# Batch 1's q and k loaded early and transposed by DMA in an attention and ResMLP kernel

## The chip, the cores and the metric

The kernel runs on one core of one Trainium2 chip. The metric is the device time of one execution in microseconds (us). Every time is a median of a kernel's executions in the fast state; the traces are of one profiled execution each, whose span is 1 to 4.4 us shorter than the median of the timed runs (the profiled run need not be the median one: for e2 and e5 it is the fastest). The core has five engines that work side by side: PE (matrix products), DVE (VectorE), ACT (ScalarE), POOL (GpSimd) and SP (which here only issues DMA). The profile counts the transfers of all of them against the same 16 DMA engines.

## The reference

Eight batches go through attention with 16 query heads and 4 key/value heads, and then through a ResMLP block whose two large weight matrices are the same for all batches.

```python
# q: (8, 16, 384, 64)   k, v: (8, 4, 384, 64)   all f32; k and v repeated 4 times
attn = softmax(q @ k^T / 8);   x = (attn @ v) as (8, 384, 1024)
a1  = alpha1 * x + beta1
tok = einsum('ts,bsd->btd', w_tok, a1)            # 384 x 384
u   = x + lam * tok
a2  = alpha2 * u + beta2
ch  = relu(a2 @ w_ch1) @ w_ch2                    # 1024 -> 4096 -> 1024
out = u + lam * ch
```

## The kernel before

The program is one long list in which the two layers of batch b (`main`) are interleaved with the attention part of batch b+1 (`side`). Batch 0's attention cannot hide behind anything and forms a prologue of some 42 us. Then comes **the first layer of batch 0** (`h`, to about 91 us), **its second layer** (`ch`, to about 142 us), the first layer of batch 1, and so on. These names are used below.

Weights of the first layer, w1, stream in for every batch in 16 chunks of 512 KiB (as bf16) through five buffers. The second layer's weights, w2, are loaded once, first 2 MB and later pieces of 256 and 512 KiB, between the w1 chunks. All of these are loads that convert f32 to bf16 and are issued by POOL:

```python
    def load_w1(n):                                     # n = 16 * batch + chunk
        if n < B * NCH:
            t = sb.tile([P, NDT, CW * P], bf, tag="w1", name="w1", bufs=RING)   # RING = 5
            c = n % NCH
            nc.gpsimd.dma_start(out=t, in_=w1src[:, :, c * CW * P:(c + 1) * CW * P])
            w1_tiles[n] = t
    # in main(b), behind chunk c of the first layer:
            load_w1(b * NCH + c + RING)
            if b == 0 and 2 <= c < 12:
                load_w2(*((0, 6 + c, 16) if c < 10 else (1, c - 10, 16)))
            if b == 0 and c == 12:
                for i in range(1, 8):
                    load_w2(1, i, 8)
```

Attention needs q and k transposed (`qT`, `kT`). There are two ways: PE multiplies by an identity matrix and an engine copies the result from PSUM, or a transposing DMA ("flip") moves it within SBUF, issued by SP:

```python
    def load_q(b, sts=range(NST)):
        if b not in qrs:
            qrs[b] = sb.tile([P, NST, Hq, D], bf, tag="q_raw", name="q_raw", bufs=1)   # one buffer
        for st in sts:
            nc.gpsimd.dma_start(out=qrs[b][:, st], in_=by_st(q[b])[:, st])

    def flip_k(b):
        nc.sync.dma_start_transpose(out=kT..., in_=k2s[b]...)        # 393 KB
    def flip_q(b):
        nc.sync.dma_start_transpose(out=qT..., in_=qrs[b]...)        # 786 KB
```

Before the change batches 0 and 1 use PE for q, k and the MLP's input a2, and batches 2 to 7 use DMA. For batches 2 and up the loads come at 55% and the flips at 85% of the main part of two batches earlier:

```python
                if not loaded and t > t_all * 0.55:
                    ...place_k(b + 2, ...); load_q(b + 2); load_v(b + 2)
                if not flipped and t > t_all * 0.85:
                    flip_k(b + 2); flip_q(b + 2)
```

Batch 0's q lies in the only `q_raw` buffer until late in the prologue, so batch 1's q cannot load earlier:

```python
        loads = {9: [(load_w1, RING - 1), (load_w2, 0, 0, 2)], 20: [(late_loads,)],   # load_k(1)
                 30: [(load_q, 1)], 37: [(load_v, 1)]}
```

The softmax here doesn't subtract the row's maximum and nothing guards it: scores larger than these inputs give would overflow.

## Time and profile before

| | before |
|---|---|
| time, median of 3 | 815.77 us (815.12 to 817.19) |
| PE busy in the span | 98% |
| first layer of batch 0 ends (first `ch` matmul) | 91.42 us |
| second layer of batch 0 ends (batch 1's first layer starts) | 141.83 us |
| waits of PE within batch 0's first layer, all together | 1.56 us |

The page of the kernel before opens with the busy time of each engine (with share of the span and number of instructions), and its third part lists the DMA queues: records, megabytes, and the time the records took as a share of the span.

```profile
PE 798.4 (98%) x6090; PEld 451.7 (55%) x6144; DVE 347.5 (43%) x678; ACT 225.0 (28%) x298; POOL 185.8 (23%) x230
...
q0 software_dynamic: 197760, 83.28, 89.8%
q1 hardware_dynamic: 62304, 28.00, 14.2%
```

PE seems to be everything here. But the share is an average over 814 us. The queue q0, which carries the weights, moves 83 MB in that time, 102 GB/s; in the prologue and in batch 0's first layer it moves about twice as much and has no pause. The last line is the queue that carries the flips and the outputs. The prediction below reads batch 0 in detail.

### The profile page before, as it was taken

What the parts mean: (1) busy time and instruction counts of PE and PEld (TensorE: products, weight loads), DVE (VectorE), ACT (ScalarE), POOL (GpSimd) and SP (SyncE); (2) the same over time, 40 slices, a digit from 0 to 9 for tenths busy, and PEclk for the clock granted to TensorE, in tenths of its full rate; (3) what the DMA queues carried; (4) which work ended last, traced back from release to release, by engine and by line L of the source; (5) the groups of instructions that cost most, each with busy time, mean ns of one, the idle gap of its engine ahead of it and who ended that gap; (6) DMA issues with size and microseconds to landing.
All of it is one profiled execution on the core that took longest, in us unless ns stands there. A gap on an engine that the chain in (4) does not pass through costs nothing.

```text
span 814.3 us, 14117 instructions
## 1 busy us (share of the span) xinstructions
PE 798.4 (98%) x6090; PEld 451.7 (55%) x6144; DVE 347.5 (43%) x678; ACT 225.0 (28%) x298; POOL 185.8 (23%) x230
## 2 busy tenths in 40 slices
PE   7999999999999999999999999999999999999997
PEld 4756555565456655566455654556555665556545
DVE  7655553344443444334442444424444244442122
ACT  4644330432113321233113331034211432102100
POOL 7244340234003240032301241022500321003000
PEclk8999999999999999999999999999999999999999
DMA  9999999999169991799947999499994998129611
GB/s 174 200 196 201 202 212 140 161 183 166 49 131 172 176 149 56 138 181 174 124 89 128 173 178 96 112 132 174 171 83 99 162 173 122 36 64 187 88 39 39
DMA packets 260670, 112.57 MB, mean 138 GB/s; under 512 B 109568, under 2 KB 254464, under 8 KB 260608
## 3 DMA queue, kind: packets, MB, share of 16 engines
q0 software_dynamic: 197760, 83.28, 89.8%
q1 hardware_dynamic: 62304, 28.00, 14.2%
q8 instruction: 48, 0.79, 0.4%
q10 hardware_dynamic: 544, 0.39, 0.2%
q14 instruction: 14, 0.11, 0.0%
HBM read 170.53 MB, written 12.58 MB: 225 GB/s over the span
## 4 chain that ended last, share of the span: by engine, by line
PE 90%; DMA 4%; DVE 4%; issue 1%; SPq 0%; POOL 0%; ACT 0%; DVEq 0%; ACTq 0%
PE ch L426 41%; PE h L399 37%; PE av L236 4%; PE sc L202 4%; PE tok L258 3%; DMA q_raw<-in_q_dram 2%; DMA w<-in_moe_w_ch_dram 2%; DVE x L242 1%; DVE hT L409 1%; DVE a1f L249 0%; DVE a L251 0%; DMA hT<-in_moe_lam_dram 0%; POOL q_raw L108 0%; SPq L472 0%; PE vec L318 0%
## 5 line engine op out<-in xcount | busy, mean ns | idle before, releaser
L399 PE MATMUL h<-a2T,w 128*128 128x384 bf16 (+1 forms) x2016 | 349.9, 326 | 1.7 <-ACT hT L407 0.5
L426 PE MATMUL ch<-w,hT 128*128 128x512 bf16 (+2 forms) x1546 | 346.1, 370 | 4.4 <-issue 0.9
L399 PEld LDWEIGHTS <-w 128*128 128x128 bf16 x2016 | 189.4, 98 | 126.3 <-issue 9.1
L126 POOL DMA_DIRECT2D w<-in_moe_w_ch_dram x128 | 112.3, 879 | 543.3 <-PE h L399 500.5
L426 PEld LDWEIGHTS <-hT 128*128 128x128 bf16 x1600 | 146.1, 98 | 153.0 <-issue 5.8
L211 ACT ACTIVATE es<-sc 128x1024 bf16<-128x1024 f32 x126 | 123.3, 1021 | 283.2 <-PE sc L202 283.2
L409 DVE TENSOR_SCALAR hT<-h,bias 128x384 bf16<-128x384 f32 x128 | 79.1, 618 | 187.0 <-PE h L399 186.5
L407 ACT ACTIVATE hT<-h,bias 128x384 bf16<-128x384 f32 x128 | 74.2, 580 | 222.1 <-PE h L399 202.6
L431 DVE TENSOR_TENSOR o<-ch,vecs 128x512 f32<-128x512 f32 (+2 forms) x50 | 33.4, 667 | 91.1 <-PE ch L426 91.1
L265 DVE TENSOR_TENSOR x<-tok,x 128x384 f32<-128x384 f32 x64 | 35.6, 556 | 80.9 <-PE tok L258 77.2
L236 PEld LDWEIGHTS <-es 128*128 128x128 bf16 x1008 | 45.8, 97 | 20.5
L236 PE MATMUL av<-v,es 128*128 128x65 bf16 x1008 | 49.0, 193 | 0.0
L202 PE MATMUL sc<-qT,kT 64*128 64x384 bf16 (+2 forms) x576 | 46.0, 275 | 0.4 <-ACT hT L211 0.3
L258 PEld LDWEIGHTS <-wtokT 128*128 128x128 bf16 x576 | 37.8, 98 | 12.6 <-issue 0.6
L241 DVE RECIPROCAL rinv<-av 128x6 f32<-128x6 f32 x64 | 12.3, 193 | 69.8 <-PE av L236 69.6
L258 PE MATMUL tok<-a,wtokT 128*128 128x128 bf16 x504 | 37.3, 219 | 0.0
L242 DVE TENSOR_TENSOR x<-av,rinv 128x384 f32<-128x384 f32 x64 | 35.7, 557 | 2.3
L202 PEld LDWEIGHTS <-kT 64*128 64x128 bf16 x576 | 20.0, 94 | 28.8 <-issue 24.6
L432 DVE TENSOR_TENSOR o<-o,x 128x512 f32<-128x512 f32 (+2 forms) x50 | 33.5, 671 | 1.7
L269 DVE TENSOR_TENSOR a<-x,vecs 128x384 bf16<-128x384 f32 x56 | 31.6, 564 | 1.9
L251 DVE TENSOR_TENSOR a<-a1f,vecs 128x384 bf16<-128x384 f32 x56 | 31.3, 558 | 2.2
L249 DVE TENSOR_TENSOR a1f<-x,vecs 128x384 f32<-128x384 f32 x56 | 31.2, 558 | 1.9
(69 smaller groups left out, 211.5 us busy)
## 6 DMA issues: line engine op xcount, KB each, us to landing
w<-in_moe_w_ch_dram POOLq DMA_DIRECT2D x135, 512.0 KB, 7.2
out_dram<-o SPq DMA_DIRECT2D x47, 256.0 KB, 2.0
q_raw<-in_q_dram POOLq DMA_DIRECT2D x21, 256.0 KB, 8.0
kst<-in_k_dram SPq DMA_DIRECT2D x16, 192.0 KB, 2.8
w<-in_moe_w_ch_dram POOLq DMA_DIRECT2D x10, 256.0 KB, 12.5
w<-in_moe_w_ch_dram POOLq DMA_DIRECT2D x1, 2048.0 KB, 21.9
v<-in_v_dram POOLq DMA_DIRECT2D x21, 64.0 KB, 7.9
a2T<-a SPq DMA_TRANSPOSE x48, 4.2
```

Of the source, the lines that this page charges most:

```text
L126: nc.gpsimd.dma_start(out=t, in_=w1src[:, :, c * CW * P:(c + 1) * CW * P])
L202: nc.tensor.matmul(out=sc[:, hh, k % 4:k % 4 + n], lhsT=kT[r, sk, 2 * p // G, :], rhs=qT[r, st:st + n, p, :], start=True, stop=True)
L211: nc.scalar.activation(out=e, in_=sc, func=EXP, scale=scale_qk)
L236: nc.tensor.matmul(out=av[:, hh, sq, :], lhsT=ess[k // 4][:, hh, k % 4, :], rhs=vb[:, sk, hk, :], start=(sk == 0), stop=(sk == NST - 1))
L242: nc.vector.tensor_tensor(out=x[:, :, cols(p)].rearrange("p st (h d) -> p h st d", h=2), in0=av[:, :, :, :D], in1=rinv.to_broadcast([P, 2, ...
L258: nc.tensor.matmul(out=ps[:, tt, :], lhsT=wtokT[:, st, tt * P:(tt + 1) * P], rhs=a1s[p][:, st, :], start=(st == 0), stop=(st == NST - 1 an ...
L265: nc.vector.tensor_tensor(out=u, in0=ps, in1=u, op=ADD)
L399: nc.tensor.matmul(out=ps[:, :n], lhsT=w1[:, dt, j * P:(j + 1) * P], rhs=a2T[:, dt, :n], start=(dt == 0), stop=(dt == NDT - 1))
L407: nc.scalar.activation(out=hT[:, nt, :], in_=ps[:, :S], func=RELU, bias=c1)
L409: nc.vector.tensor_scalar(out=hT[:, nt, :], in0=ps[:, :S], scalar1=c1, scalar2=0.0, op0=ADD, op1=mybir.AluOpType.max)
L426: nc.tensor.matmul(out=ps[:, lo:hi], lhsT=hT[:, nt, ms * P:(ms + 1) * P], rhs=w2[:, nt, dw * 512 + lo:dw * 512 + hi], start=(nt == 0), sto ...
L432: nc.vector.tensor_tensor(out=o[:, lo:hi], in0=o[:, lo:hi], in1=x[:, ms, c], op=ADD)
```

## The change

The intent is to get batch 1 ready earlier and with less work on PE. Batch 0's q goes into four separate tiles, so that `q_raw` is free at once; batch 1's k, q and v load in the prologue; its q and k are flipped by DMA, and its a2 too, as in the later batches. That takes 60 transposes from PE. Besides, LN1's scale is spread over the partitions directly in f32 rather than through a split into bf16 parts, and the early pieces stand in a new order.

```diff
@@ q_transpose
-                nc.tensor.matmul(out=ps[:, i, :], lhsT=qrs[b][:, i % NST, h:h + 2, :].rearrange("p h d -> p (h d)"),
+                nc.tensor.matmul(out=ps[:, i, :],
+                                 lhsT=qgs[h // G][:, i % NST, h % G:h % G + 2, :].rearrange("p h d -> p (h d)"),
@@ a2_transpose
-            if not pe_flip:
-                nc.sync.dma_start_transpose(...)
-                return
-            ps = tp_ps([P, NST, P])                  # (and the transposes on PE, and the copy)
+            nc.sync.dma_start_transpose(...)
@@ new
+        def spread_g1(ps_, tag):
+            ps = psum.tile([P, 4, P], f32, tag=tag, name="vec", bufs=1)
+            for i, p in enumerate(ps_):
+                nc.tensor.matmul(out=ps[:, i], lhsT=ident_f[:NP, p:p + 1].to_broadcast([NP, P]),
+                                 rhs=rows_f[:NP, :P], start=True, stop=True)
+            nc.vector.tensor_copy(out=g1[...], in_=...)
@@ side(b), b > 0
-            if pe_flip:
-                add(k_transpose, 0)
-                add(q_transpose, 0, 2, "DVE", "av")
-                add(k_transpose, 2)
-                add(q_transpose, 2, 2, "DVE", "av")
...
-                    if pe_flip and j in (1, 3):
-                        add(q_transpose, 4 + 2 * (j // 2))
@@ the end of side(0)   (the table of early pieces is also reordered: cut)
-        for f, *a in ((h_part, (0, 1), range(4)), ...
+        for f, *a in ((flip_q, 1), (place_k, 1, 0), (place_k, 1, 1), (flip_k, 1), (h_part, (0, 1), range(4)), ...
@@ prologue
-        load_q(0, [])
+        qgs = [sb.tile([P, NST, G, D], bf, tag="es", name="qg", bufs=EB) for _ in range(Hkv)]
...
-        loads = {9: [(load_w1, RING - 1), (load_w2, 0, 0, 2)], 20: [(late_loads,)], 30: [(load_q, 1)], 37: [(load_v, 1)]}
+        load_k(1)
+        load_q(1)
+        load_v(1)
+        load_w2(0, 0, 2)
```

Cut are the new order of the loads and copies of batch 0's q, the moved `spread` calls of batch 1, changes of the evicting engine and of one PSUM buffer, and `lead` 0.04 to 0.05.

More of the change, by code (lines that the diff above doesn't have):

```diff
@@ L94, in place_k @@
         copies = [nc.gpsimd.tensor_copy] * 2
-        if b == 1 or b == 0 == i:
-            copies = (nc.vector.tensor_copy, nc.vector.tensor_copy if i else nc.scalar.copy)
+        if b == 1:
+            copies = [nc.scalar.copy] * 2
+        elif b == 0 == i:
+            copies = (nc.vector.tensor_copy, nc.scalar.copy)
         for a in range(2):
@@ L163, in side @@
         first = b == 0
-        pe_flip = b < 2
         def cols(p):
@@ L253, in tok @@
         def tok(p):
-            tag, n = ("mm", 2) if first else ("av", 1) if pe_flip else ("tp", 1)
+            tag, n = ("mm", 2) if first else ("tp", 1)
             ps = psum.tile([P, NST, P], f32, tag=tag, name="tok", bufs=n)
@@ L279, in a2_transpose @@
                 return
-            if not pe_flip:
-                nc.sync.dma_start_transpose(
-                    out=a2T[:, p, :S].rearrange("p (a s) -> p a s", a=NST),
-                    in_=a2s[p].rearrange("p a d -> p (a d)"))
-                return
-            ps = tp_ps([P, NST, P])
-            for tt in range(NST):
-                nc.tensor.matmul(out=ps[:, tt, :], lhsT=a2s[p][:, tt, :], rhs=ident,
-                                 is_transpose=True, start=(tt == 0), stop=(tt == NST - 1),
-                                 skip_group_check=True)
-            nc.scalar.copy(out=a2T[:, p, :S], in_=ps.rearrange("p a b -> p (a b)"))
+            nc.sync.dma_start_transpose(
+                out=a2T[:, p, :S].rearrange("p (a s) -> p a s", a=NST),
+                in_=a2s[p].rearrange("p a d -> p (a d)"))
         def wtok_transpose(st, tag):
@@ L321, in spread @@
                       in_=ps[:, :n * w].rearrange("p (n v) d -> p n v d", n=n))
+        def spread_g1(ps_, tag):
[3 more added lines that the diff above has]
+                                 rhs=rows_f[:NP, :P], start=True, stop=True)
+            nc.vector.tensor_copy(out=g1[:, ps_[0] * P:(ps_[-1] + 1) * P], in_=ps.rearrange("p n d -> p (n d)"))
         us = []
@@ L332, in side @@
         if not first:
-            if pe_flip:
-                add(k_transpose, 0)
-                add(q_transpose, 0, 2, "DVE", "av")
-                add(k_transpose, 2)
-                add(q_transpose, 2, 2, "DVE", "av")
-                if b == 1:
-                    add(split, 2, 4)
+            if b == 1:
+                add(split, 2, 4)
+                for p in (0, 2, 4, 6):
+                    add(spread, (p, p + 1), (1, 3), "av" if p % 4 else "tp", "ACT")
+                for p in (0, 4):
+                    add(spread, range(p, p + 4), (3, 4), "av" if p else "tp", "ACT")
             for j in range(NP + 4):
@@ L345, in side @@
                     add(scores2, j)
-                    if pe_flip and j in (1, 3):
-                        add(q_transpose, 4 + 2 * (j // 2))
                 if 2 < j < NP + 3:
-                    add(tok if pe_flip else tok_flip, j - 3)
-                if pe_flip and j > 3:
-                    add(a2_transpose, j - 4)
-                if b == 1 and j < 2:
-                    for p in (4 * j, 4 * j + 2):
-                        add(spread, (p, p + 1), (1, 3), "tp", "ACT")
-                    add(spread, range(4 * j, 4 * j + 4), (3, 4), "tp", "ACT")
-                elif j < 2:
+                    add(tok_flip, j - 3)
+                if j < 2:
                     us.extend([lambda: None] * 2)
@@ L367, in side @@
         ut = a2_transpose
-        at = {1: [(warmup, 3), (split, 0, 2, 0)], 2: [(q_transpose, 2, 2, "DVE", "av"), (split, 0, 2, 1)],
-              3: [(spread, lower, (0, 1), "tp"), (wtok_transpose, 0, "av")],
-              4: [(av, 0), (wtok_transpose, 1, "tp"), (wtok_transpose, 2, "av")], 5: [(fill_h,), (rows_r, "tp")],
-              6: [(av, 1), (q_transpose, 4, 2)], 7: [(tok, 0), (k_transpose, 2)],
-              8: [(av, 2), (spread, upper, (0, 1), "av")], 9: [(tok, 1), (ut, 0)], 10: [(av, 3), (ut, 1)],
-              11: [(q_transpose, 6, 2), (tok, 2)], 12: [(tok, 3)], 13: [(av, 4), (ut, 2)], 14: [(ut, 3)],
-              15: [(tok, 4), (av, 5)], 16: [(ut, 4)], 17: [(av, 6), (tok, 5)]}
+        at = {0: [(warmup, 3)], 1: [(scale_rows,), (split, 1, 2, 0)], 2: [(q_transpose, 2, 2, "DVE", "av"), (split, 1, 2, 1)],
+              3: [(spread_g1, lower, "tp")], 4: [(wtok_transpose, 0, "av"), (av, 0), (wtok_transpose, 1, "tp")],
+              5: [(wtok_transpose, 2, "av"), (fill_h, 0), (k_transpose, 2)], 6: [(av, 1), (q_transpose, 4, 2)],
+              7: [(rows_r, "av")], 8: [(av, 2), (fill_h, 4)], 9: [(tok, 0), (spread_g1, upper, "av")],
+              10: [(tok, 1), (av, 3)], 11: [(q_transpose, 6, 2), (ut, 0), (tok, 2)], 12: [(tok, 3), (ut, 1)],
+              13: [(av, 4), (ut, 2)], 14: [(ut, 3)], 15: [(tok, 4), (av, 5)], 16: [(ut, 4)], 17: [(av, 6), (tok, 5)]}
         for i in range(18):
@@ L378, in side @@
                 add(f, *a)
-        for f, *a in ((h_part, (0, 1), range(4)), (av, 7), (ut, 5), (tok, 6),
+        for f, *a in ((flip_q, 1), (place_k, 1, 0), (place_k, 1, 1), (flip_k, 1), (h_part, (0, 1), range(4)), (av, 7), (ut, 5), (tok, 6),
                       (h_part, (2, 3), range(4)), (h_part, range(4), (4,)), (ut, 6), (tok, 7),
@@ L404, in main @@
                 if b == 0:
-                    nc.vector.tensor_copy(out=c1, in_=ps[:, S:n])
+                    evac("DVE" if nt % 2 else "ACT")(out=c1, in_=ps[:, S:n])
                 if nt % 2 == 0:
@@ L487, in place_q4 @@
         def place_q4(g, eng):
-            eng.tensor_copy(out=qrs[0][:, :, g * G:(g + 1) * G, :], in_=qhs[g].rearrange("p h st d -> p st h d"))
+            eng.tensor_copy(out=qgs[g], in_=qhs[g].rearrange("p h st d -> p st h d"))
         load_q4(1)
@@ L502, with scale_rows @@
                 nc.vector.tensor_reduce(out=t[:n], in_=ident[:n, :n].rearrange("p (k c) -> p c k", c=NP), op=ADD, axis=AX)
+        def scale_rows():
+            r = rows_f[:, :2 * P].rearrange("p (v d) -> p v d", v=2)
+            nc.vector.tensor_tensor(out=r, in0=r, in1=rows_f[:, None, 3 * P:].to_broadcast([32, 2, P]), op=MUL)
         def split(lo, hi, step=None):
             c = slice(lo * P, hi * P)
-            if lo == 0 and step != 1:
-                r = rows_f[:, c].rearrange("p (v d) -> p v d", v=2)
-                nc.vector.tensor_tensor(out=r, in0=r, in1=rows_f[:, None, 3 * P:].to_broadcast([32, 2, P]), op=MUL)
             for i, m in enumerate(masks[:2]):
@@ L517, in split, with fill_h @@
                 nc.vector.tensor_copy(out=rows_b[:32, c], in_=rows_f[:, c])
-        def fill_h():
-            nc.vector.tensor_tensor(out=H[:32].rearrange("p (n d) -> p n d", n=NP),
-                                    in0=rows_b[:32, None, P:2 * P].to_broadcast([32, NP, P]),
-                                    in1=sel4[:, :, None].to_broadcast([32, NP, P]), op=MUL)
+        def fill_h(p):
+            nc.vector.tensor_tensor(out=H[:32, p * P:(p + 4) * P].rearrange("p (n d) -> p n d", n=4),
+                                    in0=rows_b[:32, None, P:2 * P].to_broadcast([32, 4, P]),
+                                    in1=sel4[:, p:p + 4, None].to_broadcast([32, 4, P]), op=MUL)
         place_k(0, 0)
         for h, cp in ((0, nc.vector.tensor_copy), (2, nc.scalar.copy)):
-            cp(out=qrs[0][:, :, h:h + 2, :], in_=qst[:, h:h + 2].rearrange("p h st d -> p st h d"))
+            cp(out=qgs[0][:, :, h:h + 2, :], in_=qst[:, h:h + 2].rearrange("p h st d -> p st h d"))
         nc.gpsimd.tensor_copy(out=vt[0][:, :, :, :D], in_=vst.rearrange("p h st d -> p st h d"))
@@ L532 @@
         load_q4(3)
-        for c in range(RING - 1):
+        place_k(0, 1)
+        load_w1(0)
+        load_w1(1)
+        place_q4(2, nc.gpsimd)
+        place_q4(3, nc.gpsimd)
+        for c in range(2, RING):
             load_w1(c)
-        place_q4(2, nc.gpsimd)
-        place_k(0, 1)
-        place_q4(3, nc.gpsimd)
         nc.gpsimd.tensor_copy(out=a2Ts[0][:, :, S:S + 1], in_=be2[:, :, None])
-        def late_loads():
-            load_k(1)
-        loads = {9: [(load_w1, RING - 1), (load_w2, 0, 0, 2)], 20: [(late_loads,)], 30: [(load_q, 1)], 37: [(load_v, 1)]}
-        for i, f in enumerate(side(0)):
-            f()
-            for g, *a in loads.get(i, []):
-                g(*a)
-        place_k(1, 0)
-        place_k(1, 1)
+        load_k(1)
+        load_q(1)
+        load_v(1)
+        load_w2(0, 0, 2)
+        for f in side(0):
+            f()
         for b in range(B):
@@ L553 @@
             done, t, loaded, flipped = 0, 0, b + 2 >= B, b + 2 >= B
-            lead, span = (0.04, 0.82) if b == 0 else (0, 0.95)
+            lead, span = (0.05, 0.82) if b == 0 else (0, 0.95)
             if not loaded:
```

## The prediction

> **What bounds the kernel now.** I read the page first: PE is busy 98% of the span and its slices are full after the first. The chain of waits then says where PE is not the whole story. It names matmuls almost everywhere, but before 92 us it also has two long DMA pieces:
>
> ```profile
> 29.02 17.14 DMA q_raw<-in_q_dram
> 74.13 14.07 DMA w<-in_moe_w_ch_dram
> ```
>
> Columns: start, duration, what. The first piece is batch 1's q, issued late because batch 0 still held the one q_raw buffer; it landed at 46.16. The second is the last of the 16 w1 chunks of batch 0; it was 14 us on its way and landed at 88.19. The PE timeline there (start, length, instruction, idle before and its releaser) shows how little this cost:
>
> ```profile
> 45.49 0.28 PE L186 MATMUL tp<-ident,q_raw 128*128 128x128 bf16 x2
> 46.20 0.40 PE L186 MATMUL tp<-ident,q_raw 128*128 128x128 bf16 x4 [0.44 <-DMA q_raw<-in_q_dram]
> ...
> 87.58 0.33 PE L287 MATMUL tp<-ident,a 128*128 128x128 bf16 x3
> 88.24 1.48 PE L399 MATMUL h<-a2T,w 128*128 128x385 bf16 x8 [0.33 <-DMA w<-in_moe_w_ch_dram]
> ```
>
> PE waited only 0.44 and 0.33 us. A small wait at the end of a long transfer means that both sides arrive nearly together. So I asked how full the DMA is, with the table of stretches (length, then busy time of PE, PEld, DVE, ACT, POOL with counts, granted clock, DMA share, GB/s):
>
> ```profile
> 10.00:20.00 10.00, 7.11 (x77) 4.42 (x77) 8.43 (x18) 4.47 (x5) 9.63 (x12) 0.66 1.38 194
> 20.00:30.00 10.00, 9.95 (x160) 7.25 (x161) 8.13 (x18) 8.69 (x11) 3.24 (x3) 1.00 1.40 203
> ...
> 38.00:46.00 8.00, 7.75 (x61) 4.96 (x58) 3.64 (x12) 2.95 (x6) 1.81 (x3) 1.00 2.16 176
> ...
> 52.00:72.00 20.00, 19.30 (x156) 11.54 (x152) 8.59 (x26) 11.56 (x17) 9.61 (x12) 1.00 1.39 200
> 72.00:92.00 20.00, 19.54 (x187) 12.44 (x189) 11.64 (x32) 8.48 (x12) 7.83 (x10) 1.00 1.38 200
> ```
>
> The reader is to see the constant 200 GB/s from 10 us to past 90 us: the DMA is saturated through the whole prologue and batch 0's first layer. The landings of single issues confirm a queue served in order: w1 chunks 12 to 15 landed at 76.43, 80.32, 84.30 and 88.19, one per 3.95 us, which is 512 KiB of w1 plus 256 KiB of w2 (786 KB) at 199 GB/s. PE began them at 77.53, 80.93, 84.45 and 88.24. The slack shrinks from 1.1 us to nothing. Chunk 5 landed at 52.05 and was begun at 53.61, a slack of 1.6 us. **So two limits meet in batch 0's first layer: PE, and the bytes queued ahead of the last w1 chunk.** After about 143 us each batch takes 97.4 us (143.19 to 240.63 in the chain) and the change does not touch those batches.
>
> The same stretch 10 to 20 us shows a granted clock of 0.66, after a PE gap of 2.04 us at 10.02 to 12.06 (released by L517, the splitting of the f32 rows into bf16).
>
> **What the Trainium skill says.** "TensorE: Matmul & The Clock Gate", Part 1: an idle PE is put at half clock, and it takes some 3.4 us of activity to win the full clock back; the trace shows a clock of 0.50 from 14 to 18 us after the gap. Same page, "Wait — 56ns": 128 columns cost 56 ns at full clock; here three transposes step on by 0.17 us (56 ns each), though each record says 219. "DMA: Bandwidth & Descriptors", "Issuing engines are not separate DMA queues": transfers from all issuers run on the same 16 engines and interleave. The trace agrees: around the transposing DMA of one a2 block the w1 queue loses rate. The two queue tables (queue, packets, MB, share), without and with it:
>
> ```profile
> q0 software_dynamic: 1509, 0.76, 143.4%
> ```
>
> ```profile
> q0 software_dynamic: 344, 0.17, 136.2%
> q1 hardware_dynamic: 393, 0.09, 27.5%
> ```
>
> The first is 179 to 183 us (0.19 MB per us of w1). The second is 176.6 to 178.2: 0.17 MB where 0.30 would have passed. The loss of 0.13 MB is 0.7 us of DMA for one block of 98 KB; 186.5 to 188 gives 0.14 against 0.285, again 0.75 us. Alone, the big q flip ran at 208 GB/s (131 to 136 us). The same page, "Latency and other measured facts", gives 261 GB/s or more for transposing DMAs; the trace decides.
>
> **The change part by part.**
>
> (1) Removed from PE: batch 1's k and q transposes (12 + 24) and a2 transposes (24). 60 x 56 ns = 3.4 us. Of these the 36 k/q ones and one a2 group (2.2 us) lie before 91 us, in the first layer; seven a2 groups (7 x 0.17 = 1.2 us) lie in the second layer. Batch 1's work is paced by matmuls issued; counting units of the new list (44, against 54) at the half-way mark, 20 remain for the second layer: 10 half av pieces, 4 scores, 6 tok. Before it was 8, 4, 6 and the transposes. So the second layer changes by +2 x 0.275 - 1.2 = **-0.65 us**.
>
> (2) Prologue: the scale of LN1 is spread directly in f32, so the first av no longer waits for the split; scores fill the old gap. That can recover the 2.0 us gap, and half of some 7 us run at half clock (3 us): **4 to 5 us earlier start** of the first layer (42.5 now, about 38). The f32 spread's extra passes, 8 small matmuls, are about 1 us against that, inside ACT-bound time (18 exps x 1.024 us).
>
> (3) Bytes ahead of the last w1 chunk: the same w1, w2, q, k and v as before, only in another order (q, v now ahead of the first 2 MB of w2). Added: the DMA flips of q (786 KB) and k (393 KB), which the order of SyncE's instructions puts before everything of batch 0's main part, and one of the a2 flips (98 KB) before the last chunk lands. At the rate measured alone (208 GB/s) q and k cost 5.7 us; at the loss measured beside w1 (0.73 us per 98 KB) 8.8 us. I take 7.4, plus 0.7 for the a2 block: **+8 us** on the landing of chunk 15, so about 96.
>
> (4) First layer: PE starts 4 to 5 us earlier, but chunk 5 sits behind q, v, w2 and the flips and lands near 59 instead of 52. PE would reach it near 48, wait some 10 us, then follow the queue at 3.95 us per chunk. The gain of (2) and the 2.2 us of (1) are swallowed by this wait. The layer ends when chunk 15 has landed: +8 us, less the 0.33 us wait already there.
>
> (5) Batch 2's q lands behind the same backlog (129.35 now); its flip ended near 137, 5 us ahead of the scores at 142.57. With seven more a2 flips in the second layer (about 5 us of DMA) that slack is nearly used: +0 to 1 us.
>
> Sum: +7.7 - 0.65 + 0.5, about +7.5. I shade it to **+6.7, or 822.5 us**, because the flips may overlap with w1's reads better than the two small samples say.
>
> **The rivals.** (a) *PE is the bound and DMA is hidden.* Then the time falls by 2.2 + 1.2 of transposes and 4 to 5 of prologue, to about 808. For it: PE's 98%, and waits for DMA under 1 us. Against it: landings and starts that coincide for four chunks in a row, and an unbroken 200 GB/s; no part of the change takes a byte away. (b) *The flips are free*, filling gaps that w1's queue leaves. Then chunk 15 lands at 88 as before and only the -0.65 us remains: about 815. Against it: 0.7 us lost per small block. (c) *The flips cost more,* and batch 2's scores wait for qT: 827 to 830. For it: a clock loss when PE idles 10 us, and SyncE serves outputs and flips in order.
>
> **Range and chances.** The centre is the DMA-bound sum. The low end, 815, is rival (b); the high end, 829, is (c). Rival (a) has about one chance in fifteen. A change of 2% is 16.3 us; faster by that would need more than all idle and transposes of the prologue together, slower by that twice my sum.
>
> **What would show each step.** Right: chunk 15 starts at 94 to 98; the chain before it is a w1 DMA; PE has a hole of several us between 45 and 60, released by w1; 200 GB/s throughout; the second layer takes about 50 us as before (91.58 to 141.99). Step (2): the clock between 12 and 20 us is near 1 and the first-layer matmuls start near 38. Wrong: if PE shows no waits for w1 and chunk 15 starts before 86, DMA was not the bound; if chunk 15 is at 88 with both flips done, they were free.

## The result, and the profile after

The changed kernel took **828.44 us** (median of 4, 826.43 to 829.76), the kernel before 816.14 us in the same rounds. The ratio is 1.0148 (95% interval 1.0122 to 1.0175): slower by 1.5%, within the 2% that counts as the same. Every ratio here is the mean time of one kernel's fast runs over that of the other's in the same rounds, so it is not quite the ratio of the medians quoted.

| | before | after |
|---|---|---|
| first main matmul of batch 0 | 42.54 us | 42.13 us |
| sixth w1 chunk landed (number 5) | 52.05 | 58.24 |
| last w1 chunk of batch 0 landed (number 15) | 88.19 | 99.86 |
| first layer of batch 0 ends | 91.42 | 103.46 |
| second layer of batch 0 ends | 141.83 | 153.76 |
| waits of PE in batch 0's first layer | 1.56 | 14.75 |
| from there to the end | 672.42 | 673.52 |

Nearly all the loss is made before the first layer of batch 0 has ended: +12.0 us there, −0.1 us in the second layer, +1.1 us after it. The same lines of the page of the kernel after:

```profile
PE 798.2 (96%) x6038; PEld 449.0 (54%) x6092; DVE 339.8 (41%) x654; ACT 225.4 (27%) x309; POOL 184.4 (22%) x230
...
q0 software_dynamic: 197760, 83.28, 88.3%
q1 hardware_dynamic: 70304, 29.97, 16.1%
```

q0 moves the same bytes. q1 has 1.97 MB more: q (0.79), k (0.39) and eight blocks of a2 (0.79 together). PE has lost 52 instructions, but no busy time. The chain of waits after the change (start, duration, what) has these pieces of DMA beyond the prologue:

```profile
45.21 22.13 DMA w<-in_moe_w_ch_dram
67.87 16.25 DMA w<-in_moe_w_ch_dram
84.65 15.22 DMA w<-in_moe_w_ch_dram
...
149.42 5.75 DMA qT<-q_raw
```

Three w1 loads in a row carry it, where before there was one of 14 us. The timeline of PE after the change shows what they do to it (in brackets the idle time before and what ended it):

```profile
42.13 1.14 PE L391 MATMUL h<-a2T,w 128*128 128x385 bf16 x6
...
58.29 3.61 PE L391 MATMUL h<-a2T,w 128*128 128x385 bf16 x12 [6.45 <-DMA w<-in_moe_w_ch_dram]
67.39 2.79 PE L391 MATMUL h<-a2T,w 128*128 128x385 bf16 x16 [1.23 <-DMA w<-in_moe_w_ch_dram]
71.31 2.13 PE L391 MATMUL h<-a2T,w 128*128 128x385 bf16 x12 [1.14 <-DMA w<-in_moe_w_ch_dram]
...
99.91 0.83 PE L391 MATMUL h<-a2T,w 128*128 128x385 bf16 x4 [0.83 <-DMA w<-in_moe_w_ch_dram]
...
155.21 0.61 PE L204 MATMUL sc<-qT,kT 64*128 64x384 bf16 x8 [0.64 <-DMA qT<-q_raw]
```

A hole of 6.45 us ends exactly when chunk 5 has landed, and from then on PE waits for nearly every chunk. The stretches of the kernel after (columns as in the prediction):

```profile
10.00:20.00 10.00, 8.72 (x132) 6.04 (x130) 8.88 (x22) 7.92 (x9) 7.59 (x12) 1.00 1.26 182
...
52.00:72.00 20.00, 11.35 (x69) 6.17 (x70) 2.80 (x7) 5.79 (x11) 5.02 (x7) 0.83 1.30 188
72.00:92.00 20.00, 15.63 (x129) 8.61 (x127) 5.96 (x15) 7.58 (x14) 7.81 (x10) 1.00 1.38 200
```

PE did 11.35 us of work where it did 19.30 before, at a clock of 0.83, while the DMA moved 188 and 200 GB/s. What shared the DMA is seen on SP's timeline after the change:

```profile
36.68 11.96 SPq L117 DMA_TRANSPOSE qT<-q_raw  x1
48.74 7.56 SPq L113 DMA_TRANSPOSE kT<-k  x1
```

The two issues lasted 20 us together. With a quiet DMA the same instructions last 4.05 and 1.60 us (batch 2's flips before the change, at 130.99 and 129.28). The queue tables for 54 to 62 us, of the kernel before and then of the kernel after, show the sharing itself:

```profile
q0 software_dynamic: 2661, 1.59, 138.1%
```

```profile
q0 software_dynamic: 1926, 0.99, 88.5%
q1 hardware_dynamic: 1921, 0.48, 46.1%
```

**The two queues got equally many records** (1926 against 1921), and a record of a flip carries 256 bytes where one of the weights carries 512 (0.48 MB over 1921, 0.99 over 1926). So 0.48 MB of flips cost 0.60 MB of weights in these 8 us. This is what the Trainium skill, "DMA: Bandwidth & Descriptors", "Queues, rings and completion order", describes: each DMA engine takes the queue rows that have work in turn, a packet at a time. The trace agrees in so far as the counts are equal; whether a record of the trace is a packet in the page's sense, no run shows.

The flips also came with a slower DMA. Here are two lines of the DMA view of the kernel after for 40 to 68 us, the first with the rate in 40 slices of 0.7 us:

```profile
GB/s 207 195 195 196 196 194 196 200 189 174 147 139 139 126 167 189 87 13 137 183 184 181 184 183 183 182 186 180 184 184 187 188 191 169 200 232 233 240 232 200
DMA packets 10617, 5.02 MB, mean 179 GB/s; under 512 B 4790, under 2 KB 10616, under 8 KB 10616
```

The kernel before moved 5.51 MB in this stretch, 197 GB/s. So the flips not only took 1.18 MB of it, the total fell by 0.49 MB too, above all from 47 to 53 us, where the DMA came nearly to a stop (13 GB/s in one slice) with loads and a flip outstanding. The same stall stands in e2, e3, e5 and e10 (between 48 and 52 us), in every run in which an early flip ran beside loads, and not in the kernel before or in e1. Its cause is not shown.

### The profile page after: what moved, and what is told of

It is laid out like the page before. It is cut to its first block, busy times and chain, and to the rows that moved or that the text cites. A ratio compares the mean times of both kernels' runs of the same rounds, so it can differ in the third digit from the quotient of the medians.

```text
span 827.3 us, 14036 instructions
## 1 busy us (share of the span) xinstructions
PE 798.2 (96%) x6038; PEld 449.0 (54%) x6092; DVE 339.8 (41%) x654; ACT 225.4 (27%) x309; POOL 184.4 (22%) x230
## 4 chain that ended last, share of the span: by engine, by line
PE 87%; DMA 8%; DVE 3%; issue 1%; SPq 0%; ACT 0%; ACTq 0%; POOLq 0%
PE ch L418 39%; PE h L391 35%; DMA w<-in_moe_w_ch_dram 6%; PE sc L204 4%; PE av L238 4%; PE tok L260 4%; DMA qT<-q_raw 1%; DVE x L244 1%; PE h L152 1%; DMA stage<-in_q_dram 1%; PE ut L277 0%; DVE a1f L251 0%; DVE a L253 0%; DVE hT L401 0%; DVE hT L248 0%
## 5 line engine op out<-in xcount | busy, mean ns | idle before, releaser
L243 DVE RECIPROCAL rinv<-av 128x6 f32<-128x6 f32 x64 | 12.3, 193 | 66.0 <-PE av L238 66.0
```

## The experiments

Each kernel was run beside the kernel before on the same chip; all compared runs are fast. The places of time are from the profile of each. "Waits" are those of PE in batch 0's first layer; the last column is from the start of batch 1's first layer to the end. By the rule of 2%, e3 is slower, e6 unclear (its interval spans 2%), and all others count as the same as the kernel before.

| run | time, us | ratio to before (95%) | waits | first layer ends | second ends | rest |
|---|---|---|---|---|---|---|
| before | 815.77 | 1 | 1.56 | 91.42 | 141.83 | 672.42 |
| after | 828.44 | 1.0148 (1.0122–1.0175) | 14.75 | 103.46 | 153.76 | 673.52 |
| e1 no early flips | 817.36 | 1.0018 (1.0011–1.0025) | 3.81 | 90.94 | 142.45 | 672.65 |
| e2 q flipped only | 824.04 | 1.0101 (1.0077–1.0125) | 8.55 | 96.55 | 147.50 | 672.88 |
| e5 flip that nobody reads | 826.18 | 1.0120 (1.0100–1.0139) | 8.33 | 97.94 | 149.45 | 672.38 |
| e3 k flipped three times | 841.24 | 1.0310 (1.0288–1.0332) | 27.64 | 115.5 | 165.8 | 672.68 |
| e4 w2 later | 825.93 | 1.0125 (1.0109–1.0142) | 3.23 | 89.91 | 146.74 | 676.79 |
| e6 w2 in order, q2 earlier | 830.48 | 1.0182 (1.0161–1.0202) | 4.39 | 90.31 | 140.61 | 688.06 |
| e7 = e1 + e6 | 826.10 | 1.0128 (1.0111–1.0145) | 2.60 | 90.78 | 142.29 | 682.24 |
| e8 before + e6 | 823.39 | 1.0088 (1.0072–1.0103) | 1.20 | 90.50 | 140.92 | 679.35 |
| e9 e6, four w1 chunks later | 829.83 | 1.0159 (1.0138–1.0179) | 4.74 | 90.65 | 140.95 | 684.81 |
| e10 evictions on ACT | 827.28 | 1.0135 (1.0111–1.0159) | 11.48 | 101.28 | 151.58 | 673.97 |
| e11 e9, the chunks held | 823.33 | 1.0091 (1.0074–1.0107) | 3.17 | 89.61 | 139.91 | 681.81 |
| e12 before + e11 | 817.82 | 1.0022 (1.0015–1.0029) | 1.19 | 90.11 | 140.52 | 674.48 |

**The theory**: the flips' bytes go through a DMA that is full, and delay the w1 chunks queued with them. **The rivals**: the loads' new order alone does it (q, v and 2 MB of w2 ahead of the chunks); PE or the prologue does it; or SP's queue holds something else up.

### e1: the early flips undone

```diff
-      (flip_q, 1), (place_k, 1, 0), (place_k, 1, 1), (flip_k, 1), (h_part, ...
+      (place_k, 1, 0), (place_k, 1, 1), (h_part, ...
+            # b == 1: k_transpose and q_transpose on PE again, from q_raw, at the places of before
```

> The changed kernel, with batch 1's q and k turned by TensorE transposes again (36 of them), as in the kernel before; everything else of the change stays, the early loads too. Theory (the two big flips are 1.18 MB put ahead of the last w1 chunk, at one flip packet for one w1 packet): the last w1 chunk, which landed at 99.86 us with the flips and 88.19 before, lands near 91; total near 820 us, 8 to 9 below the changed kernel's 828.4. Rival A (the new order of loads, q and v ahead of w2, is what hurts): stays at 826 or above. Rival B (PE work decides): rises by 2 us to 830.

Measured: 817.36 us, 2.6 us below the expectation, with chunk 15 at 87.43 (near 91 expected). Of the 12.3 us between the kernels, 11.1 are gone, although q, k and v still load early, a2 is still flipped by DMA, and PE has 36 transposes more than in the kernel after. So the rivals that blame the order of the loads or the prologue are out for all but about 1.5 us. The largest single wait of PE in the first layer of this kernel is:

```profile
75.53 0.83 PE L397 MATMUL h<-a2T,w 128*128 128x385 bf16 x4 [1.18 <-DMA w<-in_moe_w_ch_dram]
```

### e2: only q flipped by DMA

```diff
-      (flip_q, 1), (place_k, 1, 0), (place_k, 1, 1), (flip_k, 1), ...
+      (flip_q, 1), (place_k, 1, 0), (place_k, 1, 1), ...
+            # b == 1: add(k_transpose, 0); add(k_transpose, 2)
```

> The changed kernel with only q of batch 1 flipped by DMA (786 KB); k (393 KB) turned by 12 TensorE transposes. Theory, by dose: a third of the flips' cost goes, so about 3 us less than the changed kernel: 825.5 us; last w1 chunk near 97. Rival A (order of loads): no change, 828. Rival C (it is the first flip alone, SyncE held 12 us, that matters, not the bytes): no change either, but then e1 drops.

Measured: 824.04 us, 6.7 above e1 for 786 KB; the k flip then accounts for the other 4.4 us, for 393 KB, so it is not the first flip alone (rival C). The runs of e2 and of the kernel after spread over 3.8 and 3.3 us each, so these differences are rough. What the queue tables for 40 to 68 us say of this stretch is steadier than differences of times. Of the weight queue q0 they give 5.42 MB in e1, 4.13 in e2 and 3.43 in the kernel after. The last two had 0.39 MB of batch 2's k pass in the stretch and e1 only 0.23, so 0.16 MB is set off. At the 197 GB/s of the kernel before there, the q flip displaced 1.13 MB or 5.7 us of loads, and the k flip 0.70 MB or 3.6 us.

### e5: a flip whose result nobody reads

```diff
+    def flip_idle(b):
+        nc.sync.dma_start_transpose(out=a2Ts[1].rearrange("p a (x s) -> p (a x) s", s=P),
+                                    in_=qrs[b].rearrange("p st h d -> p (st h d)"))
-      (place_k, 1, 0), (place_k, 1, 1), (h_part, ...            # e1
+      (flip_idle, 1), (place_k, 1, 0), (place_k, 1, 1), (h_part, ...
```

It is e1 with q flipped into a buffer that is idle then, while PE goes on transposing q for the use.

> The kernel of e1 (817.4 us: TensorE turns batch 1's q and k) plus one flip of batch 1's q by DMA into a buffer that nobody reads before it is overwritten. It measures the flip's traffic alone: no instruction waits for its result. Theory (786 KB more ahead of w1, one packet each in turn): as e2, 823 to 825 us, first layer's waits for w1 about 5 us longer than in e1's 3.8. Rival C (what costs is the wait of scores and of SyncE for the flips, not their bytes): 817 to 818.

Measured: 826.18 us, 8.8 above e1 and 1.2 above the expected range; that it lies 2.1 above e2 is within the spread of their runs (823.59 to 827.19 against 822.28 to 826.08). SP's and PE's timelines of this run, two lines of each answer that matter:

```profile
35.69 11.98 SPq L121 DMA_TRANSPOSE a2T<-q_raw  x1
```

```profile
56.41 1.47 PE L401 MATMUL h<-a2T,w 128*128 128x385 bf16 x4 [5.01 <-DMA w<-in_moe_w_ch_dram]
```

Nothing waits for this flip in batch 0, and still PE waits 5 us for a w1 chunk. q0 moved 3.98 MB from 40 to 68 us, against 4.13 in e2 with the flip that is used. So the cost is the traffic, not a wait for the flipped data, and not the missing transposes. SP was held here too, so this run alone does not part the bytes from a held SP; the issues of the loads do. POOL, not SP, issues w1. In the kernel after it issued chunks 5 to 9 at 42.28 to 52.19 us, no later than in the kernel before (42.69 to 53.72), and still chunk 9 landed at 75.15 instead of 64.58. This is the experiment that carries the explanation.

### e3: more of the suspected cost

```diff
-      ... (place_k, 1, 1), (flip_k, 1), (h_part, ...
+      ... (place_k, 1, 1), (flip_k, 1), (flip_k, 1), (flip_k, 1), (h_part, ...
```

> The changed kernel with the k flip of batch 1 issued three times (the same data to the same place, 786 KB more). Results stay right. Theory, by dose at 2.9 us for each k flip: last w1 chunk near 105.5, total near 834 us. If flips use otherwise idle DMA time after a point, less: 828 to 830.

Measured: 841.24 us against some 834. It missed, and the trace tells why: this was not a clean dose.

```profile
84.83 1.03 PE L204 MATMUL sc<-qT,kT 64*128 64x384 bf16 x8 [23.08 <-DMA kT<-k]
```

The three flips write the same `kT`, so batch 1's scores had to wait for the last of them, and PE did nothing else in these 23 us. The run shows another wait than the one in question, and says nothing on the size of the traffic's cost. e5 is its mended form.

### e4: half a megabyte per chunk out of the way

If the flips only displace bytes that could come later, then moving some w2 behind the last w1 chunk should take the loss back.

```diff
-            if b == 0 and 2 <= c < 12:
-                load_w2(*((0, 6 + c, 16) if c < 10 else (1, c - 10, 16)))
-            if b == 0 and c == 12:
-                for i in range(1, 8):
+            if b == 0 and 2 <= c < 10:
+                load_w2(0, c - 2, 16)
+            if b == 0 and c == 10:
+                for i in range(4, 8):
+                    load_w2(0, i, 8)
+            if b == 0 and c == 12:
+                for i in range(8):
                     load_w2(1, i, 8)
-        load_w2(0, 0, 2)
```

> The changed kernel, flips and all, with half of w2's first column half (2.1 MB) loaded behind the last w1 chunk instead of before the first layer. No byte less in all. Theory (bytes ahead of the last w1 chunk decide): that chunk lands some 10.6 us earlier, near 89, PE's waits for w1 in the first layer all but go, total near 816 or less, about 12 us below the changed kernel; the second layer may show a small wait for w2. Rival (the loss is PE, clock or semaphores of the flips): stays near 828.

Measured: 825.93 us, missed by 10. The first half came true: with less queued ahead, SP's issues of batch 1's flips lasted 3.69 and 1.48 us instead of 11.96 and 7.56, the last w1 chunk landed at 86.32 instead of 99.86, and the first layer ended at 89.91. In this run the flips moved from 37 to 44 us, at about 215 GB/s and beside no load, because the DMA had nothing else to do there: the 2 MB of w2 that fill this time in the kernel after were deferred. Then the deferred bytes were missing in their turn:

```profile
125.54 1.18 PE L421 MATMUL ch<-w,hT 128*128 128x512 bf16 x4 [2.15 <-DMA w<-in_moe_w_ch_dram]
128.06 1.87 PE L421 MATMUL ch<-w,hT 128*128 128x512 bf16 x4 [1.34 <-DMA w<-in_moe_w_ch_dram]
...
149.83 0.76 PE L204 MATMUL sc<-qT,kT 64*128 64x384 bf16 x8 [2.28 <-DMA qT<-q_raw]
```

The wait moved to w2, with a granted clock of 0.53 and 0.61 in the stretches behind those gaps (126 to 134 us), and then to batch 2's q. The Trainium skill, "TensorE: Matmul & The Clock Gate", Part 1, lets the clock of PE fall to half after an idle window of about 3.4 us. The trace agrees on the fall (0.50 from 126.3 to 133.1 us), but not on the length: the gap before it was 2.15 us.

### e6, e7, e8: the order mended further, in three kernels

Here w2's second half is ahead of the next batch's w1 chunks, and batch 2's k, q and v load from 42% instead of 55% on. e6 does this to the kernel after, e7 to e1, e8 to the kernel before.

```diff
-            load_w1(b * NCH + c + RING)
-            (w2 as in e4)
+            if b == 0 and c == 11:
+                for i in range(8):
+                    load_w2(1, i, 8)
+            load_w1(b * NCH + c + RING)
+            (w2's first half as in e4)
-                if not loaded and t > t_all * 0.55:
+                if not loaded and t > t_all * (0.55 if b else 0.42):
```

> As e4 (825.9), but with w2's second half ahead of the next batch's first two w1 chunks, and batch 2's q, k, v ahead of the following ones. e4 moved the last w1 chunk to 86.3 us as foreseen, then lost 3.5 us to w2, some 2.5 to the half clock after it and 2.3 to batch 2's qT. Theory (a single DMA queue bounds all of batch 0; each wait is a question of what stands ahead of what): these three waits go, total 815 to 817. Rival (flips' cost cannot be hidden by order): 824 or more.

> e1 with the same new order of loads. e1's PE waits 3.8 us in the first layer, all for w1; with the waits gone, 814 us (1.5 to 2 below the kernel before). If PE is bound by its own work in the first layer, 817.

> The kernel before with only the new order of loads. It waits 1.56 us in its first layer, of which about 0.7 for DMA: gain of 0.5 to 1.2 us, 814.8 us. Rival (the kernel before had DMA hidden everywhere): 815.8, no change.

Measured: 830.48, 826.10 and 823.39 us; all three missed, by 9 to 14 us. In all three the first layer and the w2 waits are mended (batch 1 starts at 140.61, 142.29 and 140.92, e6 13 us earlier than the kernel after), and in all three PE then stops at the head of batch 1, for the flip of batch 2's q. The PE timelines of e6 and of e8:

```profile
154.14 1.03 PE L204 MATMUL sc<-qT,kT 64*128 64x384 bf16 x8 [12.71 <-DMA qT<-q_raw]
```

```profile
146.99 1.04 PE L202 MATMUL sc<-qT,kT 64*128 64x384 bf16 x8 [5.26 <-DMA qT<-q_raw]
```

The waits are 12.71 (after), 7.92 (e1) and 5.26 us (before). The kernel before is hurt by the same order too, by 0.9%. This fits the view that all of batch 0, up to the flips of batch 2, is one DMA budget: its bytes have to pass by about 140 us, before the change some 5 us were to spare (batch 2's q flip ended near 137, its scores came at 142.57), and each flip that is added takes from that. But it does not show it, for these orders also waste DMA time. With the 2 MB of w2 gone from the prologue the DMA stood still, at 0 GB/s from 40 to 44 us in e7, from 37 to 42 us in e8 and from 37 to 41 us in e12 below; in e8 that is about as long as its wait. In e6, e9 and e11 the early flips ran in this hole, as in e4.

### e9 and e11: four w1 chunks behind the flips

The w1 chunks 17 to 20, which batch 1 needs only from some 144 us on, are 2.1 MB that stand ahead of batch 2's flips. e9 issues them later in program order, and loads batch 2's k, q and v from 40% on instead of 42%. e11 also ties them to the flip by a copy of one column of `qT` into the buffer that the load will fill.

```diff
 e9:
+            if b == 0 and c > 11:
+                w1_late.append(b * NCH + c + RING)
+            else:
                 load_w1(b * NCH + c + RING)
...
                     flip_q(b + 2)
+                while w1_late and t > t_all * 0.92:
+                    load_w1(w1_late.pop(0))
 e11, in load_w1(n, hold):
+            if hold:
+                nc.gpsimd.tensor_copy(out=t[:, 0, :1], in_=qT[:, 0, 0, :1])
             nc.gpsimd.dma_start(out=t, ...)
```

> The changed kernel, flips and all. Order of loads as in e6 (830.5), but four of the next batch's first five w1 chunks are issued only after batch 2's q and k flips, since they are not needed before 144 us. e6 waited 12.7 us for batch 2's qT, whose flip crawled beside those w1 chunks, and ran at half clock afterwards. Theory (in all of batch 0 the one DMA is the bound, so a load that is not needed soon must stand behind one that is): no wait for qT over 1 us, batch 1's first layer starts near 141.5, total 815 to 817, 12 us below the changed kernel with not a byte less. Rival (the flips' time is lost whatever the order, as e6 seems to say): 824 or more.

> The kernel after with e9's order of loads, and each of the four w1 chunks 17 to 20 (batch 1's second to fifth) now starts with one GpSimd copy of a column of qT into its buffer, so that its load cannot be issued before batch 2's q has been flipped. That is the wait that e9 lacked: there GpSimd issued these loads between 122.75 and 130.63 us, before the flips. Theory (the DMA bytes of batch 0 are the limit only because of the order in which they are served; 2.1 MB of w1 that nobody needs before 144 us stand ahead of the flips): the q flip lands by 139, PE's wait for qT is under 2 us, batch 1's first layer starts at 140.5 to 141.5, and the run takes 814 to 818. Rival (the flips are slow whatever is beside them, or SyncE issues them too late): a wait for qT of 5 us or more stays, 822 or more; or the held chunks come late and PE waits for w1 at 144 to 155 instead, 820 or more.

e9 took 829.83 us and missed. SP's timeline and PE's:

```profile
134.43 3.66 SPq L113 DMA_TRANSPOSE kT<-k  x1
138.25 11.14 SPq L117 DMA_TRANSPOSE qT<-q_raw  x1
```

```profile
151.47 1.04 PE L205 MATMUL sc<-qT,kT 64*128 64x384 bf16 x8 [9.71 <-DMA qT<-q_raw]
```

POOL had issued the four loads between 122.75 and 130.63 us, before the flips, because nothing held it: **a place in the program is no time**. POOL was ahead of PE, whose progress the 92% counted. So the flip ran beside w1 again, and its issue lasted 11.14 us.

e11 took 823.33 us. SP's timeline and PE's:

```profile
134.43 1.46 SPq L113 DMA_TRANSPOSE kT<-k  x1
136.06 3.90 SPq L117 DMA_TRANSPOSE qT<-q_raw  x1
```

```profile
141.85 0.61 PE L207 MATMUL sc<-qT,kT 64*128 64x384 bf16 x8 [1.12 <-DMA qT<-q_raw]
...
150.44 5.77 PE L394 MATMUL h<-a2T,w 128*128 128x384 bf16 x24 [5.93 <-DMA w<-in_moe_w_ch_dram]
```

The hold worked: the flip's issue lasted 3.90 us instead of 11.14, on the same program but for the four copies and what they wait for, and the wait for it fell from 9.71 to 1.12 us. That rules out flips that are slow by themselves. But the held chunk came only at 150.31, and PE waited 5.93 us for it. So e11 wins 5.1 us on the kernel after and stays 7.5 behind the kernel before; the expected 814 to 818 was missed in the way its own rival described.

### e12: the same order and hold in the kernel before

```diff
 the edits of e6, e9 and e11 applied to the kernel before
```

> The kernel before with the same order of loads and the same hold on w1 chunks 17 to 20 (e8 with the late chunks tied to the flip). It has no early flips of batch 1 and keeps the transposes on PE. Theory: its DMA had about 5 us to spare already, e8's wait of 5.26 us for qT goes, batch 1's first layer starts near 141, and the run takes 813.5 to 816.5; the difference to e11 then is what the change is worth when its bytes are hidden, within 2 us either way. Rival (the change itself costs time on PE or in the prologue, not through DMA): e12 is 5 us or more faster than e11.

Measured: 817.82 us, 1.3 us above the expected range, and 5.5 us faster than e11. By its number alone that is the rival's outcome (PE or the prologue), but the trace does not bear the rival out: batch 1 starts at 140.52 here and at 139.91 in e11, so up to there e11 is the faster one. The difference lies behind it, in waits for DMA. PE's longest wait in batch 1 of this kernel is

```profile
151.06 2.76 PE L402 MATMUL h<-a2T,w 128*128 128x384 bf16 x16 [1.27 <-DMA w<-in_moe_w_ch_dram]
```

against 5.93 and 1.12 us in e11: 5.8 us. Batch 2's q had landed at 126.71 (e11: 130.79) and its flip went out at 129.65 (136.06), so the held chunks were issued from 136.14 on instead of 142.46.

### e10: five evictions of the prologue moved from VectorE to ScalarE

```diff
-            nc.vector.tensor_copy(out=wtokT[:, st, :], ...)
+            (nc.scalar.copy if st else nc.vector.tensor_copy)(out=wtokT[:, st, :], ...)
-  (k_transpose, 2)   (q_transpose, 4, 2)   (q_transpose, 6, 2)
+  (k_transpose, 2, "ACT")   (q_transpose, 4, 2, "ACT")   (q_transpose, 6, 2, "ACT")
```

> The changed kernel with five PSUM evictions of the prologue (two of wtokT, one of kT, two of qT, 2.25 us of VectorE) moved to ScalarE. It tests two things. Why the prologue came out no shorter: if the unbroken VectorE chain from 13.3 to 24.8 us is what set its pace, the first layer starts 1.5 to 2 us earlier than 42.3; if ScalarE's exps set it, later than 42.3. And whether the start matters: if DMA bounds the first layer, the last w1 chunk still lands near 99.9 and the total stays within 1.5 us of 828.4, even with an earlier start; if PE bounds it, the total falls by as much as the start.

This asked why the prologue of the kernel after did not end earlier. Measured: 827.28 us, the first main matmul at 41.88 instead of 42.13. It missed: VectorE was not the only pacer. As the start hardly moved, the run does not tell what an earlier start would be worth. It tells something else: with the same flips, chunk 15 landed at 97.68 instead of 99.86, so a landing read from one profile is good to about 2 us. The gap ahead of the first `ut` transpose merely changed its releaser; the line of the kernel after, and that of e10:

```profile
24.84 0.55 PE L277 MATMUL ut<-hT,x 128*128 128x128 f32 x3 [1.18 <-DVE qT L191]
```

```profile
24.58 0.55 PE L277 MATMUL ut<-hT,x 128*128 128x128 f32 x3 [1.43 <-ACT qT L191]
```

No experiment beat the kernel before; the nearest are e1 (+0.2%) and e12 (+0.2%), both intervals just above 1.

## Why the prediction was right or wrong

The direction, the bound and the class were right; 828.44 lies at the very top of the range, 5.9 us above the number, and two of its four runs lie above 829. That the range held owes something to luck: 827 to 830 was rival (c)'s outcome. The size was off in steps (2) and (3), and the sign "200 GB/s throughout" did not come: 139 GB/s from 46 to 54 us (the prediction's own table had 176 at 38 to 46 us before the change).

- **The bound** (DMA bytes ahead of the last w1 chunk, not PE): right. e5 shows it: 786 KB of useless traffic cost 8.8 us. Rival (a), PE the bound, and rival (b), free flips, are both refuted by e1 against the kernel after: with PE relieved of 36 transposes the time rose by 11.1 us.
- **Step (1)**, −0.65 us in the second layer: measured 50.30 against 50.41, −0.1 us. The sign holds, the worth does not; no run settles where the half microsecond went.
- **Step (2)**, first layer near 38 us: wrong, 42.13. The clock from 10 to 20 us did return to 1.00 as predicted, and the 2.04 us gap is gone. What failed is the sum. The gaps between 10 and 25 us were 2.04, 0.56 and 0.28 us before (2.88) and are 0.96, 0.17 and 1.18 us after (2.31): new waits took the place of the old one. The f32 spread takes PE 1.08 us for each of its two groups (10.95 to 12.03 and 20.09 to 21.17) where the bf16 one took 0.22 and 0.32, so it costs 1.6 us, not 1. With 0.4 us gained in all, the full clock was worth about 1.4 us net, an estimate by difference (0.4 + 1.6 − 0.6), and not 3. From about 25 us to the first layer PE has no gap in either kernel, so whatever is gained must be gained before. By step (4) it would not have mattered; no run tests that.
- **Step (3)**, chunk 15 later by 8 us: right in kind, measured 11.7. The terms:
  - the two flips. From 40 to 68 us q0 moved 3.43 MB, and 5.07 in the kernel before, with the same 0.39 MB of batch 2's k beside it in both. The missing 1.64 MB is 8.3 us at 197 GB/s; against e1 it was 9.3 us (5.7 + 3.6). **The prediction had 8.8**, from the loss measured beside w1, and shaded it to 7.4 towards the rate of a flip on its own. That was the step that failed: the flips' own 1.18 MB are only part of the 1.64, the rest is the DMA's lower rate beside them.
  - the start: chunk 4 landed 1.1 us later (31.19 against 30.05).
  - the a2 block (0.7): wrong. The first one was issued at 97.40, but q1 moved nothing from 88 us until chunk 15 had landed.
  - about 1 us between chunks 10 and 11 (4.97 us apart instead of 3.95), with the DMA at 200 GB/s: 0.98 MB of loads passed there instead of 0.79.
  - These make 10.4 to 11.4 of the 11.7. A sum over all bytes closes it: until chunk 15 had landed the DMA moved 17.04 MB in 88.19 us (193.2 GB/s) before, and 18.56 MB in 99.86 us (185.9 GB/s) after. At the rate of before, the flips' 1.18 MB are 6.1 us and 0.34 MB more of other loads 1.8 us; the lower rate is the other 3.8 us. Why the rate fell, and why 0.34 MB of other loads came ahead of chunk 15, stays open.
- **Step (4)**: right. A hole of several us ends at chunk 5 (58.29, predicted near 59), then PE follows the queue; the waits grew by 13.2 us and swallowed everything else.
- **Step (5)**, 0 to 1 us at batch 2's scores: right, 0.64 us there and 1.1 us in the rest. The experiments show how thin that slack is.
- **Rival (c)**, 827 to 830, named the flips' higher cost and a wait for qT. The first came true, the second hardly; the last shading of the sum from 7.5 to 6.7 moved away from it.

Left open: whether some order hides the flips altogether. e11 removed the waits ahead of batch 1 and made a new one of 5.93 us; a hold on fewer chunks, or a later flip of a2, might lie between, but was not run; nor was an order that fills the hole which the deferred w2 left in the prologue. So "the bytes do not fit" is shown for the orders tried, not for all.

## What to carry to other kernels

A transposing DMA is not free work for PE's relief where the DMA is full: price it at the weights that fail to pass in the traces' own busy stretches, not at its rate alone. When one transfer is late on a saturated queue, reordering moves the wait to whatever comes next (here w1, then w2, then batch 2's q), so look for the stretch whose total is over its budget before moving anything, and then check that the move leaves the DMA no hole. And an issue that must stand behind another needs a dependency: an engine with nothing to wait for runs ahead of its place in the program.

## What the Trainium skill lacked or had wrong

- "DMA: Bandwidth & Descriptors", "Queues, rings and completion order", tells that the queues take turns by packet, but gives no price. In these runs a flip beside a converting load took one record for one (1921 against 1926 in 8 us), of 256 and 512 bytes; 0.48 MB of flips came with 0.60 MB less of weights, and 1.18 MB of them cost 8.3 to 9.3 us. The total rate fell too, to 139 GB/s from 46 to 54 us.
- The same page, "Latency and other measured facts", has 261 GB/s for transposing DMAs with a non-contiguous middle dimension, and more for contiguous ones. The flips of k and q, whichever case they are, ran at 208 GB/s with a quiet DMA (131 to 136 us before the change), and beside w1 at 60 GB/s (0.48 MB in 8 us).
- "Perfetto Trace Analysis" shows that an issue on SP lasts until its descriptors have been made, but neither it nor another page says how much longer that takes on a busy DMA: SP was held 11.96 us by the q flip beside w1, and 3.9 to 4.05 us with a quiet DMA, and the next output or load on SP waits behind it.
- The same page has no figure for a saturated stream of loads that convert f32 to bf16: 200 GB/s of written bytes held from 52 to 92 us in the kernel before.
- "TensorE: Matmul & The Clock Gate", Part 1, has about 3.4 us of idleness before the clock falls (cited at e4). Here gaps of 2.04 us (the kernel before, at 10.02), 2.15 and 2.28 us (e4) were each followed by a clock of 0.50; a gap of 1.64 us (the kernel after, before 84.17) was not.
